# A chunked attention and feed-forward kernel: the first product of mm2 moved into mm1, mm2's other products in a new order

## Chip, cores, metric

One core of a Trainium2 chip runs the whole program. The metric is the device time of one execution in microseconds (us); lower is better. The kernel before took 271.1 us in the median of three runs (270.4 to 271.34).

## What is computed

Attention within chunks of 64 tokens, for 8 batches of 8 heads with 576 tokens of 64 features each, and behind it a feed-forward layer with an exact GELU over the 4608 tokens, 512 to 2048 to 512 features:

```python
q_c, k_c, v_c = (a.reshape(B, H, nc, chunk, D) for a in (q, k, v))
scores = scale * np.matmul(q_c, k_c.transpose(0, 1, 2, 4, 3))
attn = softmax(scores)
x = np.matmul(attn, v_c)            # brought to (B * S, H * D)
h = x @ w_in
g = 0.5 * h * (1.0 + erf(h / sqrt(2)))
out = g @ w_out
```

Inputs and output are float32; the matrix products take bf16 and add up in float32.

## The kernel before

**Tiles.** The tokens are cut into nine tiles of 512, t = 0 to 8. Tile t < 8 holds the first 512 tokens of batch t, tile 8 the last 64 of all eight batches. Each tile goes through attention (scores S, their exp, the product AV with the values, the division by the row sums, which gives x), then mm1 (x by w_in, and GELU, which gives h), then mm2 (h by w_out, which gives y). The program is written out in one order for each engine, and the engines meet through semaphores only. While tile t is in mm2, AV of tile t+1 and S of tile t+2 are run between its products.

**Seven products.** From tile 1 on in mm1 and from tile 3 on in mm2 the products are done by Strassen's scheme in Winograd's form: seven products of half blocks instead of eight, with sums of blocks before and after. In mm1 (`mm1_groups`) this is done for four groups a, b, c, d of features, so 28 products of 4 matmuls. Their order, with what ACT and DVE do between, is a string of words (`FOUR`, L638, for tiles 3 to 8): `3b` is the third product of group b; `c1b`, `c2b`, `c3b` copy a bank of group b; `a1b`, `a2b` add its bank Z onto such a copy; `g12b` is the GELU (on ACT) of one quarter of group b, where the digits are the half of the features and the half of the rows; `h1` to `h3` are parts of the sums s1 and s2 that mm2 takes (`h_sums`). a1d and a2d are the additions of group d. g21 and the GELUs of the same half give the blocks that mm2 calls h12.

**mm2** (`mm2_seven`) makes seven products of 16 matmuls into banks X, Y, Z and W of PSUM: X = h11 by w11; its copy to Y; Y += s2 by T2; X += h12 by w21; Y += s1 by T1; Z = h22 by T4; W = s3 by T3; Y += s4 by w22. T1 to T4 are sums of w_out's blocks. Between them ACT and DVE copy or add the banks into the output rows y and into the pieces s2 (tile `y_2`) and s5 (tile `y_5`), which are copies of Y at two moments. `also(i)` inserts the attention of other tiles: `also(1)` the AV of tile t+1 (`rows_av`) and its division (`rows_x`), `also(2)` the loads of later tiles and, between the two halves of a product (`(2, 0)`) or ahead of it (tile 3), S of tile t+2 (`quad_S`) with four exps on ACT.

**ACT's tables.** Exp and GELU are in different tables of ACT. `act_table` runs a tiny activation on a scratch tile, so that the load of the table stands at that place (`ACT_TABLE_LOAD`, then an activation of `act_scratch`): Exp ahead of AV, Gelu behind the exps.

**Banks.** PSUM's eight banks are three for products (`ps_mm`), two (`ps_tp`) and three (`ps_at`) for the rest. A bank is taken in rotation: X of mm2 gets the one that mm1's group b had for its Y, Z that of group d. AV needs six banks at once: two, three and, as the last, Z of the tile in mm2 (`rows_av(n, tiles[n - 1]["Z"])`). S then reuses four of the first five.

**Queues.** All loads and stores but a few at the end are issued by SP in program order; `rows_x` issues two DMA transposes there, which bring x into the layout for mm1.

Of the kernel before, what the change touches and what calls it, by code (L numbers as in the profile page):

```python
# [11 lines left out]
def kernel(  # L12
# [10 lines left out]
    P = 128  # L23
# [328 lines left out]
    def rows_x(t):  # L352

        st = tiles[t]
        rows = work.tile([P, 2, 2 * G, 2, D], bf16, tag="x_t", name="x_r", bufs=1)
        xT = by_halves(t).rearrange("p s g (n e) -> p s (g n) e", e=P)
        for bank in range(6):
            s, b0 = bank // 3, NX * (bank % 3)
            nb = min(NX, 2 * G - b0)
            av = st["av"][bank][:, :2 * nb]  # L360
            one = work.tile([P, 2 * NX], f32, tag="one", name="one", bufs=2)
            nc.vector.reciprocal(one[:, :2 * nb], av[:, :, D])
            nc.vector.tensor_tensor(rows[:, s, b0:b0 + nb].rearrange("p b r d -> p (b r) d"), av[:, :, :D],
                                    one[:, :2 * nb].to_broadcast([P, 2 * nb, D]), op=mybir.AluOpType.mult)
            if bank % 3 == 2:
                nc.sync.dma_start_transpose(xT[:, s], rows[:, s].rearrange("p b r d -> p (b r d)"))

    def duo_banks(g2, name):
# [203 lines left out]
    def h_sums(t, j0, j1):  # L572

        a11, a12, a21, a22 = h_blocks(t, j0, j1)
        s1, s2 = h_sum(t, 1, j0, j1), h_sum(t, 2, j0, j1)
        nc.vector.tensor_tensor(s1, a21, a22, op=mybir.AluOpType.add)
        nc.vector.tensor_tensor(s2, s1, a11, op=mybir.AluOpType.subtract)
# [37 lines left out]
    def x_sums(t, which=(1, 3, 2, 4)):  # L615
# [7 lines left out]
        for i in which:  # L623
# [16 lines left out]
               g12a c1d 2b a2a g22b 6d 5c g21a a2b 2d 7c h1 g11b c3c c2d 2c g11d 5d a1c 7d c3d 3c g21b 4c g11c 3b a1d  # L640
               g22c 4d g12c g12b 3d a2c a2d g21c g22d g12d g21d h2 h3"""

    FOURS = range(FIRST7, NT)
    PROGRAMS = {1: LATE, 2: THIRD, **{t: FOUR for t in FOURS}}

    def mm1_groups(t, extra, between={}):

        st = tiles[t]
        st["h"] = hpool.tile([P, FF, MT], bf16, tag="h", name="h")
        h = st["h"][:].rearrange("p f (m e) -> p f m e", m=2)  # L650
        b11, b12, b21, b22 = x_blocks(t)
        w = in_blocks()
        TT, add = nc.vector.tensor_tensor, mybir.AluOpType.add
        banks, sums = {}, {}
        four = t in FOURS
        tags = {"a": ("y_1", "y_2"), "b": ("y_5", "rc" if four else "y_2"), "d": ("y_1", "rc")}
        first = {"a": 0, "b": 4, "c": 2, "d": 6}
        plain = [] if four else [j + FH * r for j in (6, 7) for r in range(2)]
        hs = {"h1": (0, 2), "h2": (2, 6), "h3": (6, 8)}

        def prod(g, n):
            q, e = first[g] // 4, first[g] % 4
            if n in (1, 2):
                lhs, rhs, name = w[:, n - 1, :, 0, q, e:e + 2], b11 if n == 1 else b21, "X"
            elif n == 3:
                lhs, rhs, name = w_s[g, 4], b22, "Y"
            elif n == 4:
                lhs, rhs, name = w[:, 1, :, 1, q, e:e + 2], st["T"][4], "Z"
            else:
                lhs, rhs, name = w_s[g, n - 4], st["T"][n - 4], "Z" if n == 7 else "Y"  # L670
            fresh = n in (1, 7)
            if fresh:
                pool, tag = (ps_tp, "tp") if four and name == "Z" else (ps_at, "at")
                banks[g + name] = pool.tile([P, 2, TH], f32, tag=tag, name=f"h_{name}")
            for i in range(2):
                for kk in range(2):
                    nc.tensor.matmul(banks[g + name][:, i], lhs[:, kk, i], rhs[:, kk], start=fresh and i == kk == 0,  # L677
                                     stop=(kk == 1), skip_group_check=True)

        def gelu(g, r, m):  # L680
            j = first[g] + FH * r
            src = {(0, 0): lambda: banks[g + "X"], (0, 1): lambda: banks[g + "Y"],
                   (1, 0): lambda: sums[g, 0], (1, 1): lambda: sums[g, 1]}[r, m]()
            nc.scalar.activation(h[:, j:j + 2, m], src[:], Act.Gelu)  # L684

        for word in PROGRAMS.get(t, PROGRAM).split():
            for u in extra.pop(word, ()):
                u()
            if word == "start":
                begun = mm1_slot(t, [plain.pop(0) for _ in range(4)], between, 1)  # L690
            elif word == "sums":
                x_sums(t)
            elif word == "p" and t == 1:
                begun.pop()()
            elif word == "p":
                f = plain.pop(0)
                bank = ps_tp.tile([P, MT], f32, tag="tp", name="h_ps")
                for ks in range(KS):
                    nc.tensor.matmul(bank[:].rearrange("p (s e) -> p s e", s=2), w_in_sb[:, ks, f * P:(f + 1) * P],  # L699
                                     by_halves(t)[:, :, ks] if t >= FIRSTX else  # L700
                                     st["x"][:, ks, :].rearrange("p (s e) -> p s e", s=2),
                                     start=(ks == 0), stop=(ks == KS - 1))
                nc.scalar.activation(st["h"][:, f, :], bank[:], Act.Gelu)
            elif word in hs:
                if t >= FIRST7:
                    h_sums(t, *hs[word])
            elif word[0].isdigit():
                prod(word[1], int(word[0]))
            elif word[0] == "g":
                gelu(word[3], int(word[1]) - 1, int(word[2]) - 1)  # L710
            elif word[:2] == "c1":
                g = word[2]
                banks[g + "Y"] = ps_mm.tile([P, 2, TH], f32, tag="mm", name="h_Y")
                AC(banks[g + "Y"][:], banks[g + "X"][:])  # L714
            elif word[:2] in ("c2", "c3"):
                g, i = word[2], int(word[1]) - 2
                if g != "c":
                    tag = tags[g][i]
                    sums[g, i] = work.tile([P, 2, TH], f32, tag=tag, name=f"h_{g}", bufs=2 if tag == "rc" else 1)
                elif i == 0:  # L720
                    pool, tag = (hsum, "s3") if t < B else (ypool, "y")
                    pair = pool.tile([P, 4, TH], f32, tag=tag, name="h_sb")
                    sums[g, 0] = pair[:, 0:2]
                    sums[g, 1] = pair[:, 2:4]
                (AC if i == 0 else DV)(sums[g, i][:], banks[g + "Y"][:])  # L725
            elif word[0] == "a":
                g, i = word[2], 2 - int(word[1])
                TT(sums[g, i][:], banks[g + "Z"][:], sums[g, i][:], op=add)
# [29 lines left out]
    def halves(bank):  # L758
        return [bank[:, 0], bank[:, 1]]

    def mm2_seven(t, at={}):

        def also(i):
            for u in at.get(i, ()):
                u()
        st = tiles[t]
        h = st["h"][:].rearrange("p (k f) (m e) -> p k f m e", k=2, m=2)
        w = w_out_sb[:].rearrange("p (k f) (n e) -> p k f n e", k=2, n=2)
        T = [None] + [w_t[i] for i in range(1, 5)]
        def bank_mm():  # L770
            return ps_mm.tile([P, 2, NH], f32, tag="mm", name="y_ps")
        X, Y = bank_mm(), bank_mm()
        s2, s5 = (work.tile([P, 2, NH], f32, tag=nm, name=nm, bufs=1) for nm in ("y_2", "y_5"))
        y = [ypool.tile([P, 2, d_model], f32, tag="y", name="y_sb") for _ in range(2)]
        TT, add = nc.vector.tensor_tensor, mybir.AluOpType.add
        if t == B:
            s1 = work.tile([P, 2, NH], f32, tag="y_1", name="y_1", bufs=1)
            last_seven(t, h, w, T, (X, Y, bank_mm()), (s1, s2, s5), y)
            return
        also(0)  # L780
        product(halves(X), h[:, 0, :, 0], w[:, 0, :, 0], True)
        AC(Y[:], X[:])  # L782
        Z = bank_mm()
        st["Z"] = Z[:].rearrange("p m n -> p (m n)")
        also(1)
        h_third(t)
        product_by_f(halves(Y), h_sum(t, 2), T[2])
        AC(s2[:], Y[:])
        product(halves(X), h[:, 1, :, 0], w[:, 1, :, 0], False)
        AC(y[0][:, :, :NH], X[:])  # L790
        store(t, 0, 0, y)
        product(halves(Y), h_sum(t, 1), T[1], False)
        AC(s5[:], Y[:])
        h_fourth(t)
        also(2)
        product(halves(Z), h[:, 1, :, 1], T[4], True, lambda m: also((2, m)))
        TT(s2[:], Z[:], s2[:], op=add)
        also(3)
        W = bank_mm()
        product(halves(W), h_sum(t, 3), T[3], True)  # L800
# [164 lines left out]
    with tc.manual_schedule():  # L965
# [126 lines left out]
        for t in range(1, NT):  # L1092
# [30 lines left out]
            elif n < NT:  # L1123
# [58 lines left out]
                    e2[4] += [next_k]  # L1182
                if n + 1 < NT:
                    e2[1] = [lambda: act_table(Act.Exp)] + e2[1]
                    e2.setdefault(2 if t == FIRST7 else (2, 0), []).extend([lambda: quad_S(n + 1), lambda: act_table(Act.Gelu)])
            phase(t, e1, e2, between=last_rows if t == 1 else {})
# [1 line left out]
_INS = ['q', 'k', 'v', 'moe_w_in', 'moe_w_out']  # L1188
# [26 lines left out]
```

## Time and profile before

| | us |
|---|---|
| median of three runs | 271.1 |
| lowest, highest | 270.4, 271.34 |
| the profiled execution, device time | 270.41 |
| its span, first to last instruction | 268.6 |
| tile 4, from its first product of mm1 to that of tile 5 | 134.66 to 160.93 |
| mean clock granted to TensorE | 0.996 of full speed |

PE is TensorE's matmuls, PEld its loads of weights, DVE VectorE, ACT ScalarE, POOL GpSimd, SP the engine that issues DMAs. A row of a timeline has its start and its length in us, the engine, the line of the kernel, the operation, output<-inputs, shape and count; in brackets the time that the engine sat idle before, and who ended it. Rows of equal kind that follow each other are merged. In the chain of waits the program is followed back from its last instruction, each step to what released it.

### The profile page before, as it was taken

To read this page: it belongs to the slowest core of one execution; us is meant where nothing else is said; L and a number is where in the kernel's file an instruction comes from. 1 tells how busy PE (TensorE), PEld (TensorE's weight loads), DVE (VectorE), ACT (ScalarE), POOL (GpSimd) and SP (SyncE) were. 2 spreads that over 40 slices of the span, in tenths; PEclk is the share of its full clock that TensorE was granted. 3 is DMA by queue.
4 is the path that set the end of the run, shared out by engine and by line. 5 is a ranking of instruction groups with operands and counts; after the bars stand their busy time and mean duration, and the time that the engine had idled before them with its cause. 6 is when DMAs were issued, how large, how long until landed. Compare 5 with 4: busy or idle time off the path is not lost.

```text
span 268.6 us, 7554 instructions
## 1 busy us (share of the span) xinstructions
PE 259.6 (97%) x3077; PEld 195.6 (73%) x3092; DVE 202.1 (75%) x372; ACT 187.1 (70%) x364; POOL 77.0 (29%) x130
## 2 busy tenths in 40 slices
PE   7989999999999999999999999999999999999993
PEld 3554454476548654888888888888888888888882
DVE  2565775989997879589569956995699769958961
ACT  3466756797767967897689669957995799239700
POOL 3735667361440061441044103500362030000000
PEclk9999999999999999999999999999999999999998
DMA  7999999997979959999899989988886760430005
GB/s 230 285 377 402 395 388 243 237 286 194 336 205 261 244 123 231 279 237 191 232 232 231 177 216 242 264 152 206 237 193 146 166 192 0 89 138 12 2 2 156
DMA packets 127075, 56.59 MB, mean 211 GB/s; under 512 B 103488, under 2 KB 120896, under 8 KB 127040
## 3 DMA queue, kind: packets, MB, share of 16 engines
q1 hardware_dynamic: 126592, 55.59, 79.4%
q10 hardware_dynamic: 448, 0.52, 0.7%
q8 instruction: 24, 0.39, 0.6%
q14 instruction: 11, 0.09, 0.1%
HBM read 36.70 MB, written 9.44 MB: 172 GB/s over the span
## 4 chain that ended last, share of the span: by engine, by line
PE 92%; ACT 2%; DVE 1%; DMA 1%; issue 1%; POOL 0%; SPq 0%; ACTq 0%; DVEq 0%; POOLq 0%
PE y_ps L746 24%; PE h_Y L677 15%; PE y_ps L866 12%; PE h_Z L677 10%; PE h_X L677 10%; PE h_ps L538 6%; PE y_ps L891 4%; PE y_ps L755 4%; PE s_ps L247 2%; PE h_ps L699 1%; DMA arrival<-in_k_dram 1%; PE tp L170 1%; ACT y_ps L782 1%; PE warm L958 1%; PE rc_ps L484 1%
## 5 line engine op out<-in xcount | busy, mean ns | idle before, releaser
L677 PEld LDWEIGHTS <-w_in_s 128*128 128x128 bf16 x480 | 46.8, 98 | 6.1
L677 PEld LDWEIGHTS <-w_in_sb 128*128 128x128 bf16 x360 | 35.1, 98 | 6.5
L677 PE MATMUL h_X<-x,w_in_sb 128*128 128x256 bf16 x240 | 33.7, 272 | 0.0
L677 PE MATMUL h_Y<-x_t,w_in_s 128*128 128x256 bf16 x240 | 32.7, 272 | 0.0
L866 PE MATMUL y_ps<-w_out_sb,h 128*128 128x512 bf16 x137 | 31.7, 379 | 0.9 <-issue 0.8
L746 PEld LDWEIGHTS <-h_s 128*128 128x128 bf16 x304 | 29.7, 98 | 3.6 <-issue 0.2
L746 PEld LDWEIGHTS <-h 128*128 128x128 bf16 x288 | 27.8, 98 | 3.4
L218 POOL CAST v_nat<-arrival 128x1024 bf16<-128x1024 f32 x14 | 14.8, 1061 | 48.4 <-DMA arrival<-in_v_dram 48.3
L164 POOL CAST q_nat<-arrival 128x512 bf16<-128x512 f32 x33 | 19.4, 627 | 28.2 <-DMA arrival<-in_q_dram 19.1
L164 POOL CAST k_nat<-arrival 128x512 bf16<-128x512 f32 x34 | 21.9, 678 | 14.0 <-DMA arrival<-in_k_dram 10.1
L746 PE MATMUL y_ps<-w_t,h_s 128*128 128x256 bf16 x208 | 24.8, 273 | 0.0
L866 PEld LDWEIGHTS <-h 128*128 128x128 bf16 x144 | 13.3, 98 | 15.0 <-issue 0.2
L746 PE MATMUL y_ps<-w_out_sb,h 128*128 128x256 bf16 x192 | 22.9, 273 | 0.0
L963 ACT ACT_TABLE_LOAD x16 | 20.5, 1283 | 1.0 <-PEq L1199 0.7
L684 ACT ACTIVATE h<-h_Y 128x512 bf16<-128x512 f32 x30 | 17.7, 595 | 2.4 <-PE h_Y L677 1.9
L714 ACT COPY h_Y<-h_X 128x512 f32<-128x512 f32 x30 | 17.0, 582 | 2.8 <-PE h_X L677 2.6
L684 ACT ACTIVATE h<-h_X 128x512 bf16<-128x512 f32 x30 | 17.8, 597 | 1.4 <-PE h_X L677 0.6
L677 PE MATMUL h_Z<-x_t,w_in_s 128*128 128x256 bf16 x120 | 18.0, 273 | 0.0
L677 PE MATMUL h_Y<-x,w_in_s 128*128 128x256 bf16 x120 | 17.7, 273 | 0.0
L677 PE MATMUL h_Z<-x_t,w_in_sb 128*128 128x256 bf16 x120 | 17.4, 272 | 0.0
L725 DVE COPY h_a<-h_Y 128x512 f32<-128x512 f32 x8 | 5.5, 692 | 14.1 <-PE h_Y L677 14.1
L254 ACT ACTIVATE pT<-s_ps 128x512 bf16<-128x512 f32 x28 | 14.5, 601 | 2.3 <-PE s_ps L247 2.3
(148 smaller groups left out, 489.4 us busy)
## 6 DMA issues: line engine op xcount, KB each, us to landing
arrival<-in_q_dram SPq DMA_DIRECT2D x7, 1024.0 KB
arrival<-in_k_dram SPq DMA_DIRECT2D x24, 256.0 KB
out_dram<-y_sb SPq DMA_DIRECT2D x23, 256.0 KB
arrival<-in_v_dram SPq DMA_DIRECT2D x20, 256.0 KB
arrival<-in_moe_w_out_dram SPq DMA_DIRECT2D x4, 1024.0 KB
arrival<-in_v_dram SPq DMA_DIRECT2D x30, 128.0 KB
out_dram<-y_sb SPq DMA_DIRECT2D x5, 512.0 KB
arrival<-in_moe_w_in_dram SPq DMA_DIRECT2D x4, 512.0 KB
```

The costliest lines, as they stand in the source:

```text
L164: copy(st[nm][:, g].rearrange("p j r d -> p r j d"), st[nm + "f"][:, 2 * g:2 * g + 2])
L218: copy(st["v"][:, part[0], part[1], :D], st["vf"][:, part[0], part[1]])
L254: nc.scalar.activation(pT[:].rearrange("p u (c j) -> p u c j", j=J), s_ps[g2][c][:].rearrange("p u (j c) -> p u c j", j=J), Act.Exp, scale ...
L538: nc.tensor.matmul(h_ps[a][:], w_in_sb[:, ks, f * P:(f + 1) * P], st["x"][:, ks, :], start=(ks == 0), stop=(ks == KS - 1))
L677: nc.tensor.matmul(banks[g + name][:, i], lhs[:, kk, i], rhs[:, kk], start=fresh and i == kk == 0, stop=(kk == 1), skip_group_check=True)
L684: nc.scalar.activation(h[:, j:j + 2, m], src[:], Act.Gelu)
L714: AC(banks[g + "Y"][:], banks[g + "X"][:])
L746: nc.tensor.matmul(out[m], lhs[:, f, m * P:(m + 1) * P], rhs[:, f, :], start=fresh and f == 0 and (m == 0 or len(out) == 3), stop=(f == FH ...
L755: nc.tensor.matmul(out[m], lhs[:, f, m * P:(m + 1) * P], rhs[:, f, :], start=False, stop=(f == FH - 1), skip_group_check=True)
L866: nc.tensor.matmul(y_ps[:], st["h"][:, f, ms * P:(ms + 1) * P], w_out_sb[:, f, :], start=(f == 0), stop=(f == FF - 1))
L891: nc.tensor.matmul(tiles[t]["y_ps", ms][:], tiles[t]["h"][:, f, ms * P:(ms + 1) * P], w_out_sb[:, f, :], start=(f == 0), stop=False)
L963: nc.scalar.activation(act_scratch[:], rest[:, 0:1], func)
```

## The change

It touches tiles 3 to 7 (tile 8 keeps its order).

- **mm1's words.** A new string `AHEAD` stands for `FOUR`. It differs in its last third: 3b comes ahead of 3c, then 4c, and then `X`, the whole product h11 by w11 of mm2 (16 matmuls), ahead of 4d and 3d. `cX` copies X to Y on ACT, behind g21c. On DVE the sums of `h2` come ahead of a2d.
- **mm2's order.** PE's products were X, AV, Y += s2 T2, X += h12 w21, Y += s1 T1, Z (with S between its halves), W, Y += s4 w22. Now they are X += h12 w21, AV, Y += s2 T2, Z, Y += s1 T1 (with S between its halves, in tile 3 too), W, Y += s4 w22. The store of the first half of y now comes ahead of the transposes on SP.
- **rows_x** reads AV's banks in the order 5, 3, 4, 0, 1, 2 instead of 0 to 5, and so issues the transpose of the second half of the rows first.

```diff
-        for bank in range(6):
+        for at, bank in enumerate((5, 3, 4, 0, 1, 2)):
...
-            if bank % 3 == 2:
+            if at % 3 == 2:
                 nc.sync.dma_start_transpose(xT[:, s], rows[:, s].rearrange("p b r d -> p (b r d)"))
...
+    AHEAD = """begin 1a 1b c1a 1c 6a 7a c1b c2a 6b 5a 2a c1c 6c c2b 5b 7b c3a g11a a1a c3b c2c 3a a1b 1d 4a g22a 4b
+               g12a c1d 2b a2a g22b 6d 5c g21a a2b 2d 7c h1 g11b c3c c2d 2c g11d 5d a1c 7d c3d 3b g21b g11c 3c a1d
+               g22c 4c g12b X g12c a2c 4d g22d g21c cX h2 a2d 3d g12d g21d h3"""
...
-    PROGRAMS = {1: LATE, 2: THIRD, **{t: FOUR for t in FOURS}}
+    PROGRAMS = {1: LATE, 2: THIRD, **{t: AHEAD if t < B else FOUR for t in FOURS}}
...
+            elif word == "X":
+                mm2_first(t)
+            elif word == "cX":
+                st["Y"] = bank_mm()
+                AC(st["Y"][:], st["X"][:])
...
+    def mm2_first(t):
+        h, w = out_blocks(t)
+        tiles[t]["X"] = bank_mm()
+        product(halves(tiles[t]["X"]), h[:, 0, :, 0], w[:, 0, :, 0], True)
+
     def mm2_seven(t, at={}):
...
-        X, Y = bank_mm(), bank_mm()
+        X, Y = (st["X"], st["Y"]) if t < B else (bank_mm(), bank_mm())
...
-        also(0)
-        product(halves(X), h[:, 0, :, 0], w[:, 0, :, 0], True)
-        AC(Y[:], X[:])
         Z = bank_mm()
         st["Z"] = Z[:].rearrange("p m n -> p (m n)")
+        product_by_f(halves(X), h[:, 1, :, 0], w[:, 1, :, 0])
+        AC(y[0][:, :, :NH], X[:])
+        store(t, 0, 0, y)
         also(1)
-        h_third(t)
         product_by_f(halves(Y), h_sum(t, 2), T[2])
         AC(s2[:], Y[:])
-        product(halves(X), h[:, 1, :, 0], w[:, 1, :, 0], False)
-        AC(y[0][:, :, :NH], X[:])
-        store(t, 0, 0, y)
-        product(halves(Y), h_sum(t, 1), T[1], False)
-        AC(s5[:], Y[:])
+        product(halves(Z), h[:, 1, :, 1], T[4], True)
+        h_third(t)
+        TT(s2[:], Z[:], s2[:], op=add)
         h_fourth(t)
         also(2)
-        product(halves(Z), h[:, 1, :, 1], T[4], True, lambda m: also((2, m)))
-        TT(s2[:], Z[:], s2[:], op=add)
+        product(halves(Y), h_sum(t, 1), T[1], False, lambda m: also((2, m)))
+        AC(s5[:], Y[:])
         also(3)
...
-                    e2.setdefault(2 if t == FIRST7 else (2, 0), []).extend([lambda: quad_S(n + 1), lambda: act_table(Act.Gelu)])
+                    e2.setdefault((2, 0), []).extend([lambda: quad_S(n + 1), lambda: act_table(Act.Gelu)])
```

ACT in mm2 of tile 4, before (y_2 is s2, y_5 is s5, pT are the exps of S, y_sb the output rows; y_ps are banks X and Y):

```order
L782 COPY y_ps_2706<-y_ps_2705 128x512
L963 ACT_TABLE_LOAD
L963 ACTIVATE act_scratch_113<-rest_58 128x1
L788 COPY y_2_2707<-y_ps_2706 128x512
L790 COPY y_sb_2709<-y_ps_2705 128x2x256
L793 COPY y_5_2708<-y_ps_2706 128x512
L254 ACTIVATE pT_2968<-s_ps_2900 128x512
L254 ACTIVATE pT_2970<-s_ps_2901 128x512
L254 ACTIVATE pT_2972<-s_ps_2902 128x512
L254 ACTIVATE pT_2974<-s_ps_2903 128x512
L963 ACT_TABLE_LOAD
L963 ACTIVATE act_scratch_113<-rest_58 128x1
```

The same place with the change (line numbers are the changed file's):

```order
L801 COPY y_sb_2726<-y_ps_2686 128x2x256
L978 ACT_TABLE_LOAD
L978 ACTIVATE act_scratch_113<-rest_58 128x1
L805 COPY y_2_2724<-y_ps_2711 128x512
L254 ACTIVATE pT_2968<-s_ps_2900 128x512
L254 ACTIVATE pT_2970<-s_ps_2901 128x512
L254 ACTIVATE pT_2972<-s_ps_2902 128x512
L254 ACTIVATE pT_2974<-s_ps_2903 128x512
L978 ACT_TABLE_LOAD
L978 ACTIVATE act_scratch_113<-rest_58 128x1
L812 COPY y_5_2725<-y_ps_2711 128x512
L821 COPY y_sb_2726<-y_ps_2711 128x2x256
```

The copy of X to Y has left (it stands between two GELUs of mm1 now), and the copy into y_5 has gone from ahead of the exps to behind the table load and its scratch activation.

DVE at the end of mm1 of tile 4, before (h_d is group d's piece, h_sb group c's; h_s1 and h_s2 are the sums s1 and s2):

```order
L728 TENSOR_TENSOR h_sb_2590<-h_Z_2634,h_sb_2590 128x512
L728 TENSOR_TENSOR h_d_2650<-h_Z_2662,h_d_2650 128x512
L576 TENSOR_TENSOR h_s1_2639<-h_2513 128x1024
L577 TENSOR_TENSOR h_s2_2640<-h_s1_2639,h_2513 128x1024
L576 TENSOR_TENSOR h_s1_2639<-h_2513 128x512
L577 TENSOR_TENSOR h_s2_2640<-h_s1_2639,h_2513 128x512
L362 RECIPROCAL one_2800<-av_ps_2730 128x6
```

And with the change:

```order
L737 TENSOR_TENSOR h_sb_2590<-h_Z_2634,h_sb_2590 128x512
L576 TENSOR_TENSOR h_s1_2639<-h_2513 128x1024
L577 TENSOR_TENSOR h_s2_2640<-h_s1_2639,h_2513 128x1024
L737 TENSOR_TENSOR h_d_2650<-h_Z_2662,h_d_2650 128x512
L576 TENSOR_TENSOR h_s1_2639<-h_2513 128x512
L577 TENSOR_TENSOR h_s2_2640<-h_s1_2639,h_2513 128x512
L362 RECIPROCAL one_2818<-y_ps_2728 128x4
```

a2d (h_d_2650) has gone behind the two sums of `h2`, and the first bank that the division reads is now Z (y_ps_2728).

More of the change, by code (lines that the diff above doesn't have):

```diff
@@ L759, in halves, with bank_mm, out_blocks @@
         return [bank[:, 0], bank[:, 1]]
+    def bank_mm():
+        return ps_mm.tile([P, 2, NH], f32, tag="mm", name="y_ps")
+    def out_blocks(t):
+        return (tiles[t]["h"][:].rearrange("p (k f) (m e) -> p k f m e", k=2, m=2),
+                w_out_sb[:].rearrange("p (k f) (n e) -> p k f n e", k=2, n=2))
+    def mm2_first(t):
+        h, w = out_blocks(t)
+        tiles[t]["X"] = bank_mm()
+        product(halves(tiles[t]["X"]), h[:, 0, :, 0], w[:, 0, :, 0], True)
     def mm2_seven(t, at={}):
@@ L766, in mm2_seven @@
         st = tiles[t]
-        h = st["h"][:].rearrange("p (k f) (m e) -> p k f m e", k=2, m=2)
-        w = w_out_sb[:].rearrange("p (k f) (n e) -> p k f n e", k=2, n=2)
+        h, w = out_blocks(t)
         T = [None] + [w_t[i] for i in range(1, 5)]
-        def bank_mm():
-            return ps_mm.tile([P, 2, NH], f32, tag="mm", name="y_ps")
-        X, Y = bank_mm(), bank_mm()
+        X, Y = (st["X"], st["Y"]) if t < B else (bank_mm(), bank_mm())
         s2, s5 = (work.tile([P, 2, NH], f32, tag=nm, name=nm, bufs=1) for nm in ("y_2", "y_5"))
```

## The prediction

> **What bounds the kernel now.** I read the page's busy times and its chain that ended last, then the table of stretches (one per tile), then the timelines of PE, ACT and DVE for tile t = 4, the second of the five that change.
>
> ```profile
> PE 259.6 (97%) x3077; PEld 195.6 (73%) x3092; DVE 202.1 (75%) x372; ACT 187.1 (70%) x364; POOL 77.0 (29%) x130
> PE 92%; ACT 2%; DVE 1%; DMA 1%; issue 1%; POOL 0%; SPq 0%; ACTq 0%; DVEq 0%; POOLq 0%
> 134.70:161.00 26.30, 26.25 (x355) 23.09 (x353) 20.22 (x41) 20.68 (x37) 7.05 (x12) 1.00 1.02 212
> 213.60:239.10 25.50, 25.45 (x290) 22.53 (x289) 20.13 (x41) 15.64 (x29) 2.10 (x2) 1.00 0.37 93
> ```
>
> The first two rows say that PE is the bound: 92% of the chain is PE. The other two are stretches (start:end, length, then busy time of PE, PEld, DVE, ACT, POOL, then granted clock, DMA share, GB/s): PE is busy 26.25 of 26.30 us at clock 1.00. So nothing is to be won by filling large holes; a change gains tenths by closing small gaps, and it loses whatever new wait it puts in front of PE. ACT is busy for only 20.68 us, so what matters on ACT is the order, not the sum.
>
> The PE timeline of t = 4 (start, length, line, operation):
>
> ```profile
> 144.81 0.60 PE L677 MATMUL h_Y<-x,w_in_s 128*128 128x256 bf16 x4
> 145.24 0.60 PE L677 MATMUL h_Z<-x_t,w_in_sb 128*128 128x256 bf16 x4
> 145.68 0.60 PE L677 MATMUL h_Y<-x,w_in_s 128*128 128x256 bf16 x4
> 146.18 0.60 PE L677 MATMUL h_Z<-x_t,w_in_sb 128*128 128x256 bf16 x4
> 146.61 0.60 PE L677 MATMUL h_Y<-x,w_in_s 128*128 128x256 bf16 x4
> 147.05 1.91 PE L746 MATMUL y_ps<-w_out_sb,h 128*128 128x256 bf16 x16
> 148.89 0.60 PE L347 MATMUL av_ps<-v_nat,pT 64*64 64x65 bf16 x50
> ...
> 149.67 1.91 PE L755 MATMUL y_ps<-w_t,h_s 128*128 128x256 bf16 x16
> 154.91 1.04 PE L746 MATMUL y_ps<-w_t,h 128*128 128x256 bf16 x8
> 155.88 0.74 PE L247 MATMUL s_ps<-q_t,k_t 64*64 64x64 bf16 x64
> 156.55 1.05 PE L746 MATMUL y_ps<-w_t,h 128*128 128x256 bf16 x8
> 157.43 1.91 PE L746 MATMUL y_ps<-w_t,h_s 128*128 128x256 bf16 x16
> 159.18 1.91 PE L746 MATMUL y_ps<-w_out_sb,h_s 128*128 128x256 bf16 x16
> ```
>
> Starts give the pace: a product of mm1 (4 matmuls) takes 0.435, one of mm2 (16) takes 1.75 (157.43 to 159.18), so a matmul 0.109. A length is longer than the pace because matmuls overlap. Gaps: 3b to 4d is 0.50 in place of 0.44; the scores S cost 0.76 (from 154.91 + 0.875 = 155.79 to 156.55); AV costs 0.87 (147.05 + 1.75 = 148.80 to 149.67).
>
> **The change part by part.** I work in the frame of this tile: nothing of mm1 moves before 144.81.
>
> *What it may gain.* Before, AC(Y<-X) stands between X and the product on Y:
>
> ```profile
> 145.44 0.60 ACT L684 ACTIVATE h<-h_Y 128x512 bf16<-128x512 f32 x1
> 146.32 0.60 ACT L684 ACTIVATE h<-h_Y 128x512 bf16<-128x512 f32 x1 [0.28 <-PE h_Y L677]
> 147.85 0.59 ACT L684 ACTIVATE h<-h_Y 128x512 bf16<-128x512 f32 x1
> 148.33 0.63 ACT L684 ACTIVATE h<-h_d 128x512 bf16<-128x512 f32 x1
> 149.05 0.57 ACT L782 COPY y_ps<-y_ps 128x512 f32<-128x512 f32 x1
> ```
>
> The copy ends at 149.62 and the product on Y starts at 149.67: PE had finished AV and waited. With X and its copy in mm1 that wait goes. AV should then cost what S costs, whose 64 matmuls are as many: 0.76, so 0.11 a tile (bounds 0 and 0.15). The 0.06 ahead of 4d goes too: 4d overwrites the bank that a1d reads until 146.12 (DVE rows below), and X now stands between them.
>
> *X inside mm1.* The order is 3b 3c 4c X 4d 3d, so 3b starts at 144.81, 3c at 145.24, 4c at 145.68, X at 146.12. X's bank was group b's, which g12b reads: 3b ends at 144.81 + 0.60 = 145.41, g12b starts 0.03 later as the second ACT row does after its product (145.68 + 0.60 = 146.28), and ends at 146.04. X is not held (0.03 to spare once 0.05 for the signal is counted, 149.62 to 149.67). X runs to 147.87, 4d to 148.31, 3d to 148.75.
>
> *The product onto X, now first in mm2* (h12 by w21, at 148.75). It needs two things early. First the copy of X: X's last matmul ends at 146.12 + 1.91 = 148.03, the copy started 0.09 after that end before (147.05 + 1.91 = 148.96, 149.05), so it runs 148.12 to 148.69 and releases PE at 148.74, just in time. Second, from its 13th matmul on (148.75 + 12 x 0.109 = 150.06), g21d, which waits for a2d on DVE, which now stands behind the sums of h2:
>
> ```profile
> 145.43 0.69 DVE L728 TENSOR_TENSOR h_d<-h_Z,h_d 128x512 f32<-128x512 f32 x1
> 146.04 0.68 DVE L728 TENSOR_TENSOR h_sb<-h_Z,h_sb 128x512 f32<-128x512 f32 x1
> 147.42 0.68 DVE L576 TENSOR_TENSOR h_s<-h 128x1024 bf16<-128x1024 bf16 x1
> 148.14 0.69 DVE L577 TENSOR_TENSOR h_s<-h_s,h 128x1024 bf16<-128x1024 bf16 x1
> 149.54 0.19 DVE L362 RECIPROCAL one<-av_ps 128x6 f32<-128x6 f32 x1
> 153.07 0.42 DVE L363 TENSOR_TENSOR x_r<-y_ps,one 128x256 bf16<-128x256 f32 x1
> 153.41 1.21 DVE L581 TENSOR_TENSOR h_s<-h 128x2048 bf16<-128x2048 bf16 x1
> 159.44 0.69 DVE L801 TENSOR_TENSOR y_sb<-y_ps,y 128x512 f32<-128x512 f32 x1 [1.04 <-PE y_ps L746]
> 160.64 0.75 DVE L625 TENSOR_TENSOR x_t<-x 128x512 bf16<-128x512 bf16 x2
> ```
>
> a2c waits for 4c (ends 146.28) and runs to 147.01; h2 takes the next 1.33 (147.42 to 148.75 in these rows), to 148.26; a2d needs 4d's end, 147.87 + 0.60 = 148.47, and runs to 149.20. On ACT, g12d waits for 3d (ends 148.91), starts at 148.94, and g21d follows at the usual step of 0.48 (147.85 to 148.33), 149.42 to 150.05. With 0.05 for the signal and 0.11 for the weights, the 13th matmul starts at 150.21 and not 150.06: **0.15 lost**. Bounds: 0 (ACT a little ahead) and 0.7 (a2d late by one more DVE operation).
>
> So AV starts 0.15 later, ends 0.11 faster, and 0.06 is already won: S stands where it stood, 155.88, and the five tiles win or lose nothing here: -0.02 each.
>
> *Reading the banks.* The twelve operations of rows_x keep their 3.87 (149.54 to 153.41) but start after AV's end, about 151.4, and end at 155.3. Bank 5 is free at 152.0, the product on Z comes at 153.16. S reuses banks that are read by 154.6, before 155.88. The third sum then ends at 156.5 (wanted 157.43), the fourth, behind one addition more, at 158.3 (wanted 159.18). All covered; by 0.9 at the least.
>
> *s5: the copy that changes its place.* Before, AC(s5<-Y) ran ahead of the exps. Now Y's product with s1 is the one around S, so in ACT's order its copy stands behind the four exps, the load of the Gelu table and the scratch activation:
>
> ```profile
> 155.11 0.59 ACT L793 COPY y<-y_ps 128x512 f32<-128x512 f32 x1 [1.16 <-PE y_ps L746]
> 156.38 2.06 ACT L254 ACTIVATE pT<-s_ps 128x512 bf16<-128x512 f32 x4 [0.68 <-PE s_ps L247]
> 158.46 1.28 ACT L963 ACT_TABLE_LOAD   x1
> 159.76 0.20 ACT L963 ACTIVATE act_scratch<-rest 128x1 f32<-128x1 bf16 x1
> 77.00 0.20 ACT L963 ACTIVATE act_scratch<-rest 128x1 f32<-128x1 bf16 x1
> 77.11 1.05 ACT L877 COPY y_sb<-y_ps 128x512 f32<-128x512 f32 x2
> ```
>
> S starts at 155.88 as before, so exps, load and scratch keep these times. The last two rows, from an earlier tile, show that a copy starts 0.11 after the scratch's start: s5 runs 159.87 to 160.46. The last product of the tile adds onto Y, so it may not start before Y is read: 160.51 and not 159.18. **PE waits 1.33**, in the tiles that have an S here (t = 3 to 6; t = 7 has no tile left to score and no table to load). Behind it on ACT stand the last copy and next tile's copies of X, which wait for PE anyway; on DVE the two additions to y and x_sums start at 160.5, not 159.44, and give T2 some 2.3 later (1.20 from the first addition to x_sums in the rows above, then three sums), at 162.8; PE wants it after the last product and three of mm1, 160.51 + 1.75 + 1.31 = 163.6. Nothing is added to the wait, and nothing gives it back: mm1 that follows is PE-bound (25.45 of 25.50 in the tile without S). Bounds: 1.22 (first exp 0.1 sooner) and 1.45.
>
> The Trainium skill, "ScalarE: Activation LUTs", section "What ACT_TABLE_LOAD costs", puts a switch of sets at about 1283 ns of load and 1380 ns of drain. By it the wait would be 1.33 + 1.38 = 2.71 and the sum four times 1.38, 5.5, larger. The load agrees with the row 158.46; of the drain the rows 159.76 and 77.11, which follow at once, show nothing.
>
> *Sum:* 4 x 1.33 - 5 x 0.02 = +5.2. Profiled execution: 270.4 (span 268.6, 1.8 around it) to 275.6. The median before, 271.1, lies 0.7 above that execution; **I predict 276.3**.
>
> **Rivals.**
> *The wait does not decide (other side).* The place is Y's last product in t = 3 to 6. Its copy must end 3.25 after S's start and ends 4.58 after it; the difference is the table load, 1.28, almost exactly. If the load ran beside the exps, or the copy came ahead of it, the wait would be 0.05. With g21d in time too, the tiles would win 0.17 each: 271.1 + 0.2 - 0.9 = 270.4. For it speaks only that ACT has idle time; against it that load and exps stand one behind another in the rows, as everything on ACT does.
> *g21d later than worked out.* From about 0.15, each tenth is paid five times. At the bound of 0.7, 276.3 + 5 x 0.55 = 279.0. The chain has four handovers between ACT and DVE, which speaks for something; but it starts from 4c, early.
> *The transposes of x become late.* They wait for rows_x, so come 1.9 later:
>
> ```profile
> 147.89 1.20 SPq L144 DMA_DIRECT2D arrival<-in_v_dram  x2
> 151.63 3.50 SPq L366 DMA_TRANSPOSE x<-x_r  x2
> ```
>
> Issued by 155.13, they had landed at 160.64, when x_sums started unheld: within 5.5. Now they are out by 157.0 and wanted at 161.7 (160.64 plus the 1.0 that DVE starts later): 4.7. If the whole 5.5 is needed, 0.8 in four tiles and up to 1.9 in the fifth: 276.3 + 5.1 = 281.4 at most, 278.5 at half. SP idles ahead of them (149.09 to 151.63), which speaks against a queue. The loads behind them come 1.9 later too, a tile or more before use.
> *The table load stalls ACT after it as well.* If it took as long again as its row, 1.28, the wait would be 2.61 four times: 281.4. The rows 77.00 and 77.11 speak against it. This is where the page of the skill points.
>
> **How the numbers follow.** Forecast 0.82; g21d clearly later 0.07; transposes 0.04; long load 0.02; no wait at Y 0.05. The forecast's own range is 4 x (1.22 to 1.45) with the tile's small terms from -0.17 to +0.25 five times, +4.0 to +7.0: 275.1 to 278.1. With the medians' own scatter (270.4 to 271.34) and part of the second rival, 274.7 to 278.3 holds 8 in 10. What a measurement here can tell from no change is about 0.3%, 0.8 us. Faster 0.03 and same 0.03, nearly all from the rival on the other side; slower 0.94.
>
> **What would show it.** Right: in t = 3 to 6 a PE gap of about 1.3 ahead of the last product on Y, released by the ACT copy into y_5, which starts right after the scratch activation; none in t = 7; the copy of X off the chain of waits; a gap of 0.1 to 0.2 within the first product of mm2. Wrong: that copy ahead of the exps, a gap after the load, x_sums waiting for DMA, or tiles no longer than 26.3.

## The result, and the profile after

| | before | after |
|---|---|---|
| median of six runs, us | 271.35 | 275.44 |
| lowest, highest, us | 270.4, 272.55 | 274.41, 277.25 |
| ratio of the times, 95% interval | 1 | 1.0156 [1.0116, 1.0197] |
| profiled execution, us | 270.41 | 275.05 |
| its span, us | 268.6 | 273.3 |

By the medians the kernel became slower by 4.1 us; the interval of the ratio makes it 3.1 to 5.3 us. Against the prediction (276.3, range 274.7 to 278.3) the time came out 0.9 lower and inside the range.

The page after, its busy times and the shares of its chain that ended last:

```profile
PE 260.1 (95%) x3077; PEld 194.6 (71%) x3092; DVE 202.6 (74%) x372; ACT 187.2 (69%) x364; POOL 77.5 (28%) x130
PE 77%; SPq 9%; DMA 5%; ACT 4%; issue 2%; POOL 2%; DVE 0%; POOLq 0%
```

PE's busy time grew by 0.5 us only (259.6 before), while the span grew by 4.7: the time went into PE standing still, not into more work. That the chain gives 9% to SP's queue looks like a new bound, but most of it is one place: followed back from the end, the chain leaves PE in tile 6 through a k_t that came late (below), and from there runs over POOL's casts of k and along the issue of loads in SP's queue from 199.83 back to 184.99. The table by tile says more. Its columns are start:end, length, busy time of PE, PEld, DVE, ACT and POOL, the granted clock, DMA share and GB/s; the tiles are cut at their first product of mm1. After the change:

```profile
107.82:135.31 27.49, 26.35 (x353) 22.92 (x352) 20.00 (x38) 20.35 (x37) 6.79 (x11) 1.00 0.97 227
135.31:162.82 27.51, 26.37 (x355) 22.93 (x353) 20.27 (x40) 20.67 (x37) 7.07 (x12) 1.00 0.91 209
...
190.33:218.19 27.86, 26.43 (x355) 22.90 (x353) 20.76 (x40) 20.66 (x37) 8.15 (x14) 1.00 0.91 184
218.19:243.68 25.49, 25.49 (x290) 22.20 (x288) 19.98 (x39) 15.74 (x29) 2.10 (x2) 1.00 0.33 85
sum 135.86, PE 131.01 PEld 113.88 DVE 101.25 ACT 98.09 POOL 30.01; mean PE 26.20 PEld 22.78 DVE 20.25 ACT 19.62 POOL 6.00
```

The same cut before the change:

```profile
108.40:134.66 26.26, 26.21 (x354) 23.05 (x352) 19.54 (x37) 20.26 (x37) 6.86 (x11) 1.00 0.99 236
...
187.19:213.53 26.34, 26.29 (x354) 22.96 (x352) 21.43 (x40) 20.68 (x37) 8.34 (x14) 1.00 0.75 183
sum 130.62, PE 130.39 PEld 114.65 DVE 101.34 ACT 97.94 POOL 30.11; mean PE 26.08 PEld 22.93 DVE 20.27 ACT 19.59 POOL 6.02
```

Tiles 3, 4 and 5 (27.49, 27.51, 27.51) are 1.23 to 1.25 longer, tile 6 is 1.52 longer, and tile 7, the one without scores to compute, has its old 25.49. The sum is +5.24. The two profiled executions differ by less, 4.64, because in the one of after the tiles begin 0.58 earlier (107.82 for 108.40). The program is unchanged up to there, so that part is scatter between executions.

Where it goes within a tile is in PE's timeline of t = 4 after the change:

```profile
146.33 0.60 PE L681 MATMUL h_Z<-x_t,w_in_sb 128*128 128x256 bf16 x4
146.77 1.91 PE L755 MATMUL y_ps<-w_out_sb,h 128*128 128x256 bf16 x16
...
149.39 1.98 PE L764 MATMUL y_ps<-w_out_sb,h 128*128 128x256 bf16 x16
151.30 0.60 PE L347 MATMUL av_ps<-v_nat,pT 64*64 64x65 bf16 x50
...
152.00 1.92 PE L764 MATMUL y_ps<-w_t,h_s 128*128 128x256 bf16 x16
...
156.47 0.74 PE L247 MATMUL s_ps<-q_t,k_t 64*64 64x64 bf16 x64
157.14 2.79 PE L755 MATMUL y_ps<-w_t,h_s 128*128 128x256 bf16 x24
161.07 1.91 PE L755 MATMUL y_ps<-w_out_sb,h_s 128*128 128x256 bf16 x16 [1.14 <-ACT y L812]
```

The row of 24 matmuls is the second half of Y's product and all of W's. At the prediction's pace, 1.75 for 16 matmuls, it is done at 157.14 + 24 x 0.1094 = 159.77, and the last product onto Y starts at 161.07: PE waits 1.30 (the bracket's 1.14 counts only from the end of the last matmul). The same bracket stands in t = 3, 4, 5 and 6, and nowhere else. ACT in the same stretch, and then the chain of waits there:

```profile
156.97 2.06 ACT L254 ACTIVATE pT<-s_ps 128x512 bf16<-128x512 f32 x4 [2.38 <-PE s_ps L247]
159.05 1.28 ACT L978 ACT_TABLE_LOAD   x1
160.35 0.20 ACT L978 ACTIVATE act_scratch<-rest 128x1 f32<-128x1 bf16 x1
160.46 0.57 ACT L812 COPY y<-y_ps 128x512 f32<-128x512 f32 x1
```

```profile
156.54 0.45 PE s_ps L247 x30
156.98 2.05 ACT pT L254 x4
...
160.55 0.48 ACT y L812
161.07 1.91 PE y_ps L755 x16
```

Y's product was complete by about 158.2 (157.14 and its eight matmuls, 0.875, with the overlap), yet the copy that frees Y has four exps and a table load ahead of it in ACT's order. It does not need either of them; it merely stands behind them. PE leaves its own work at the scores, goes through ACT and comes back 1.30 late.

### The profile page after: what moved, and what is told of

It reads as the page before. It is cut to its first block, busy times and chain, and to the rows that moved or that the text cites. A ratio compares the mean times of both kernels' runs of the same rounds, so it can differ in the third digit from the quotient of the medians.

```text
span 273.3 us, 7553 instructions
## 1 busy us (share of the span) xinstructions
PE 260.1 (95%) x3077; PEld 194.6 (71%) x3092; DVE 202.6 (74%) x372; ACT 187.2 (69%) x364; POOL 77.5 (28%) x130
## 4 chain that ended last, share of the span: by engine, by line
PE 77%; SPq 9%; DMA 5%; ACT 4%; issue 2%; POOL 2%; DVE 0%; POOLq 0%
PE y_ps L755 15%; PE h_Y L681 13%; PE y_ps L881 11%; PE h_Z L681 9%; PE h_X L681 8%; PE h_ps L538 5%; PE y_ps L764 5%; PE y_ps L906 4%; DMA arrival<-in_moe_w_in_dram 3%; SPq L106 2%; ACT pT L254 2%; DMA k_t<-k_nat 2%; SPq L149 2%; SPq L111 2%; PE s_ps L247 2%
## 5 line engine op out<-in xcount | busy, mean ns | idle before, releaser
L881 PEld LDWEIGHTS <-h 128*128 128x128 bf16 x144 | 13.4, 98 | 15.0 <-issue 0.2
L755 PEld LDWEIGHTS <-h 128*128 128x128 bf16 x208 | 20.4, 98 | 2.3
L978 ACT ACT_TABLE_LOAD x16 | 20.5, 1283 | 1.0 <-PEq L1214 0.7
L681 PE MATMUL h_Y<-x,w_in_s 128*128 128x256 bf16 x120 | 16.9, 272 | 0.0
L755 PE MATMUL y_ps<-w_out_sb,h_s 128*128 128x256 bf16 x96 | 11.4, 272 | 4.6 <-ACT y L812 4.6
```

The source lines that it names most:

```text
L755: nc.tensor.matmul(out[m], lhs[:, f, m * P:(m + 1) * P], rhs[:, f, :], start=fresh and f == 0 and (m == 0 or len(out) == 3), stop=(f == FH ...
L881: nc.tensor.matmul(y_ps[:], st["h"][:, f, ms * P:(ms + 1) * P], w_out_sb[:, f, :], start=(f == 0), stop=(f == FF - 1))
L978: nc.scalar.activation(act_scratch[:], rest[:, 0:1], func)
```

## The experiments

Each kernel was timed beside the kernel before on the same chip, whose median over those runs was 270.72 (17 runs, first four experiments) and 270.52 (23 runs, last four). Diffs are against the changed kernel where nothing else is said.

**1. The table load behind the copy.** If the 1.28 of the load are the whole loss, putting the load behind the copy of s5 must give everything back.

```diff
-                    e2.setdefault((2, 0), []).extend([lambda: quad_S(n + 1), lambda: act_table(Act.Gelu)])
+                    e2.setdefault((2, 0), []).append(lambda: quad_S(n + 1))
+                    e2[3].append(lambda: act_table(Act.Gelu))
```

> The changed kernel with the Gelu table's load (and its scratch activation) moved behind the copy of s5; the copy still stands behind the four exps. Theory (the load ahead of the copy is what holds Y's last product): copy ends about 3.7 after S starts less the 0.6 that exps leave, that is at 159.6 in the changed kernel's tile 4, before PE comes at 159.77; the four waits of 1.30 go, tiles 3 to 5 take 26.2 each, 275.4 - 5.2 = 270.3. In tile 6 S also waits for k_t (0.36 in the changed kernel); that chain runs over SP and POOL and does not shorten, so there up to 1.3 of the gain may come back: up to 271.6. Rival (the exps, or the fourth sum on DVE, hold it): 274 or more, and a gap before Y's last product stays.

Measured: 270.47 us (12 runs), ratio to before 0.9998 [0.9968, 1.0028]. ACT and PE of t = 4 in this kernel:

```profile
156.04 2.06 ACT L254 ACTIVATE pT<-s_ps 128x512 bf16<-128x512 f32 x4 [2.38 <-PE s_ps L247]
157.97 0.62 ACT L812 COPY y<-y_ps 128x512 f32<-128x512 f32 x1
158.60 1.28 ACT L978 ACT_TABLE_LOAD   x1
```

```profile
156.21 2.79 PE L755 MATMUL y_ps<-w_t,h_s 128*128 128x256 bf16 x24
158.84 1.91 PE L755 MATMUL y_ps<-w_out_sb,h_s 128*128 128x256 bf16 x16
```

The copy ends at 158.59, the product onto Y follows its predecessor without a bracket (156.21 + 2.63 = 158.84), and tiles 3 to 7 add up to 130.61 us, where before had 130.62. So the order of the load and the copy is all of the loss, and the rest of the change together is worth nothing that can be measured (the interval is -0.9 to +0.8 us).

**2. Two more switches in the same place.** This stretches the disputed cost, and asks whether a load holds ACT longer than its row says.

```diff
-                    e2.setdefault((2, 0), []).extend([lambda: quad_S(n + 1), lambda: act_table(Act.Gelu)])
+                    e2.setdefault((2, 0), []).extend([lambda: quad_S(n + 1), lambda: act_table(Act.Gelu),
+                                                      lambda: act_table(Act.Exp), lambda: act_table(Act.Gelu)])
```

> The changed kernel with one more switch to Exp and one more to Gelu (two loads and two scratch activations) between the exps and the copy of s5, in tiles 3 to 6. Theory: each adds its own rows, 1.28 + 0.20 + 0.03 = 1.5, so the wait grows from 1.30 to 4.3 and the time by 4 x 3.0 = 12.0, to 287.4. Rival of a load that also stalls ACT after it (1.38 more each by the Trainium skill's figure, ScalarE: Activation LUTs, What ACT_TABLE_LOAD costs): 4 x 5.8 = 23, to 298.5. If the copy did not decide: 275.4.

Measured: 294.9 us (2 runs), ratio 1.0887 [1.0826, 1.0947], 7.5 more than forecast. ACT of t = 3 with the extra switches:

```profile
131.72 1.28 ACT L978 ACT_TABLE_LOAD   x1
133.01 0.20 ACT L978 ACTIVATE act_scratch<-rest 128x1 f32<-128x1 bf16 x1
133.23 1.28 ACT L978 ACT_TABLE_LOAD   x1
...
134.75 1.28 ACT L978 ACT_TABLE_LOAD   x1
136.04 0.20 ACT L978 ACTIVATE act_scratch<-rest 128x1 f32<-128x1 bf16 x1
136.15 0.57 ACT L812 COPY y<-y_ps 128x512 f32<-128x512 f32 x1
```

Each switch, load and scratch, takes 1.51 (131.72, 133.23, 134.75), with nothing behind the load that holds ACT. PE's row, and the windows of its wait and of the product behind:

```profile
136.77 3.49 PE L755 MATMUL y_ps<-w_out_sb,h_s 128*128 128x256 bf16 x16 [4.17 <-ACT y L812]
```

```profile
132.50:136.70 4.20, 0.10 (x1) 0.00 (x0) 0.00 (x0) 4.13 (x7) 0.00 (x0) 1.00 1.05 313
136.70:140.10 3.40, 3.33 (x17) 2.32 (x17) 3.32 (x6) 0.02 (x1) 2.56 (x4) 0.53 0.69 157
```

The row of 24 matmuls ahead starts at 129.80, so the wait is 136.77 - 132.43 = 4.34, which is 1.30 + 2 x 1.52. That part is as expected. What the expectation left out is the granted clock, the third number from the right: 1.00 during the wait, 0.53 in the stretch after it. The last product then takes 3.28 (136.77 to 140.05) in place of 1.75. With 1.61, 1.45 and 1.61 in the other three tiles that is 6.2. In t = 4 and 6 the slow stretch reaches into mm1 as well, as its first row behind t = 4 shows (1.47 at full clock):

```profile
172.32 2.51 PE L681 MATMUL h_X<-x,w_in_sb 128*128 128x256 bf16 x12
```

By their starts, these 12 matmuls take 1.04 longer behind t = 4, 0.79 behind t = 6 and 0.13 behind t = 3, 2.0 together. Tiles 3 to 7 add up to 155.97, 20.1 more than after the change: 12.0 for the switches, 6.2 and 2.0 for the clock.

**3. The banks read in their old order.** This undoes `rows_x` alone, to see what the reversal is for.

```diff
-        for at, bank in enumerate((5, 3, 4, 0, 1, 2)):
+        for at, bank in enumerate(range(6)):
```

> The changed kernel with rows_x reading AV's banks in the order 0 to 5 again. Theory: the product on Z, due 1.75 after AV, now waits for the last of twelve DVE operations (3.9 from AV's end) and not for the first two (0.6): about 2.0 in each of five tiles, 285.4, with the wait for s5 unchanged at 1.3. Rival (DVE gets there in any case, since it can start on bank 0 before AV is over): 276 to 278.

Measured: 286.18 us (2 runs), ratio 1.0565 [1.0506, 1.0623]; the forecast is 0.8 off. In t = 4 the product on Z waits for the last read of AV's last bank:

```profile
158.85 1.91 PE L755 MATMUL y_ps<-w_t,h 128*128 128x256 bf16 x16 [1.85 <-DVE x_r L363]
```

The product ahead starts at 155.07, so it was due at 156.82: 2.03 lost. Without that bank read first, Z in the middle of mm2 costs 2 us a tile. The edit costs all five tiles, t = 7 as well, as this wait does not hang on the scores.

**4. The kernel before with its copy of s5 late.** The mechanism alone, without anything else of the change: one line of the kernel before moves behind the product on Z, which puts it behind the scores' exps.

```diff
         product(halves(Y), h_sum(t, 1), T[1], False)
-        AC(s5[:], Y[:])
...
         product(halves(Z), h[:, 1, :, 1], T[4], True, lambda m: also((2, m)))
+        AC(s5[:], Y[:])
```

> The kernel before with one line moved: the copy of s5 goes behind the product on Z, so that on ACT it stands behind the exps, the Gelu load and the scratch activation, as the change has it. Everything else as before. Theory: this alone makes nearly all of the loss. In tiles 4 to 6 S stands as far ahead of Y's last product as in the change: 1.30 each; in tile 3 S comes one half product earlier, so 1.30 - 0.87 = 0.43; sum 4.3, to 275.6. Rival (the loss comes from the order of PE or from late transposes): 271.3.

Measured: 274.34 us (5 runs), 3.6 over before, ratio 1.0136 [1.0097, 1.0175]. PE and then ACT of t = 4:

```profile
156.58 1.91 PE L746 MATMUL y_ps<-w_t,h_s 128*128 128x256 bf16 x16
159.62 1.91 PE L746 MATMUL y_ps<-w_out_sb,h_s 128*128 128x256 bf16 x16 [1.13 <-ACT y L796]
```

```profile
159.00 0.57 ACT L796 COPY y<-y_ps 128x512 f32<-128x512 f32 x1
```

The product was due at 156.58 + 1.75 = 158.33 and starts 1.29 later. Tiles 3 to 6 grow by 0.41, 1.28, 1.30 and 1.21; in t = 3 the scores still stand ahead of the product on Z, so the copy has more time. With experiment 1 this closes the case from both sides: the copy behind exps and load makes the loss without the change, and the change with the load moved behind the copy makes none.

**5. The load behind the copy, and g21d ahead of g12d.** The first experiment with the one other small loss removed, as a candidate that could beat both. The edit of experiment 1 is in it too; shown is what it adds.

```diff
-               g22c 4c g12b X g12c a2c 4d g22d g21c cX h2 a2d 3d g12d g21d h3"""
+               g22c 4c g12b X g12c a2c 4d g22d g21c cX h2 a2d 3d g21d g12d h3"""
```

> The changed kernel with the Gelu load behind the copy of s5, and on ACT g21d ahead of g12d. Theory: g21d is then issued at a2d's end (149.87 in the changed kernel's tile 4) and not behind g12d (150.08), and ends 0.2 earlier, so the 0.07 that PE loses at the 13th matmul of the first product of mm2 goes in each of five tiles: 0.3 less than with the load moved alone, about 270.1 against 270.5; tiles 26.13. Too little for the times to settle; the tiles' lengths in the trace should show it. Rival: g12d, now later, holds the sums of h3 or AV's last bank, and the gap comes back there: tiles 26.2 or longer.

Measured: 270.53 us (12 runs), ratio 1.0003 [0.9977, 1.0029]. The table by tile of this kernel, its sum:

```profile
sum 130.17, PE 130.10 PEld 114.29 DVE 101.78 ACT 98.01 POOL 29.39; mean PE 26.02 PEld 22.86 DVE 20.36 ACT 19.60 POOL 5.88
```

The five tiles take 0.45 less than before (t = 3, 5 and 6 take 26.12 to 26.14; t = 4 takes 26.35, as X starts 0.2 late there). mm2's first product isn't held any more (149.20 to 151.04 in t = 4, its pace and the 0.09 in front of AV), but the gain is within the scatter of the times (269.95 to 272.05). No version tried here is faster than before.

**6. One more switch.** Between the wait of 1.3 that leaves the clock alone and the one of 4.3 that does not.

```diff
-                    e2.setdefault((2, 0), []).extend([lambda: quad_S(n + 1), lambda: act_table(Act.Gelu)])
+                    e2.setdefault((2, 0), []).extend([lambda: quad_S(n + 1), lambda: act_table(Act.Sqrt),
+                                                      lambda: act_table(Act.Gelu)])
```

> The changed kernel with one more table load (a square root on the scratch tile) between the exps and the Gelu load, in tiles 3 to 6. PE's wait becomes 1.30 + 1.5 = 2.8 (4.3 with two more loads, after which the granted clock fell to 0.53 for some 3 us). Theory: the wait alone is paid, 275.4 + 4 x 1.5 = 281.4, if the clock stays at 1.00 after 2.8; if the clock already falls after 2.8, some 1.7 more in the tiles where it does, up to 288.

Measured: 288.32 us (2 runs), ratio 1.066 [1.0588, 1.0732]. The wait is 2.8 (a bracket of 2.66, where 1.14 stands for 1.30). PE's rows of t = 3 and 4:

```profile
138.07 1.91 PE L755 MATMUL y_ps<-w_out_sb,h_s 128*128 128x256 bf16 x16 [2.66 <-ACT y L812]
167.19 3.37 PE L755 MATMUL y_ps<-w_out_sb,h_s 128*128 128x256 bf16 x16 [2.66 <-ACT y L812]
```

The windows of the second of these products and of what comes behind it:

```profile
167.20:170.40 3.20, 3.20 (x16) 2.26 (x16) 3.20 (x5) 0.00 (x0) 2.67 (x4) 0.53 1.20 270
170.40:173.00 2.60, 2.60 (x26) 2.31 (x24) 0.65 (x2) 2.14 (x5) 0.00 (x0) 1.00 0.76 173
```

After the first wait of 2.8 the product has its usual length, 1.91, and so the full clock; after the second it has 0.53, and 1.00 again 3.2 us later. In t = 5 and 6 it is as in t = 4 (lengths of 3.49 and 3.44). The tiles are 10.8 longer than after the change, and 4 x 1.5 for the loads with 1.46, 1.57 and 1.53 for the three slow products make 10.6. The profiled execution has 2.8 more ahead of tile 3, where the program is unchanged; what it is was not settled. Why the first of the four waits left the clock alone is taken up at the end.

**7. Only X moved into mm1.** mm2's remaining products go back to before's order, with s5 copied ahead of the scores.

```diff
-        product_by_f(halves(X), h[:, 1, :, 0], w[:, 1, :, 0])
-        AC(y[0][:, :, :NH], X[:])
-        store(t, 0, 0, y)
         also(1)
+        h_third(t)
         product_by_f(halves(Y), h_sum(t, 2), T[2])
...
-        product(halves(Z), h[:, 1, :, 1], T[4], True)
-        h_third(t)
-        TT(s2[:], Z[:], s2[:], op=add)
+        product(halves(X), h[:, 1, :, 0], w[:, 1, :, 0], False)
+        AC(y[0][:, :, :NH], X[:])
+        store(t, 0, 0, y)
+        product(halves(Y), h_sum(t, 1), T[1], False)
+        AC(s5[:], Y[:])
         also(2)
-        product(halves(Y), h_sum(t, 1), T[1], False, lambda m: also((2, m)))
-        AC(s5[:], Y[:])
+        product(halves(Z), h[:, 1, :, 1], T[4], True, lambda m: also((2, m)))
+        TT(s2[:], Z[:], s2[:], op=add)
```

> Only X and its copy stand in mm1 (with the new order of words and of banks); behind it mm2's products in the order of before: AV first, then s2, X by h12, s1 with its copy ahead of S, Z around S. Theory: no wait for s5, so the loss goes: the gain of the copy hidden in mm1 (0.08) and of the gap ahead of 4d (0.06) stands against AV, which now comes straight behind 3d and waits some 0.2 for a2d and g12d on two of its banks: 271.3, within 0.8. Rival (moving X in itself costs the time): 274 to 276.

Measured: 271.74 us (10 runs), ratio 1.0053 [1.0018, 1.0087]: a small loss. Tiles 3 to 6 take 105.93 us, 0.8 more than before (130.62 - 25.49 = 105.13). AV, now straight behind mm1, takes 1.00 in t = 4:

```profile
150.01 0.82 PE L347 MATMUL av_ps<-v_nat,pT 64*64 64x65 bf16 x50
...
151.01 1.92 PE L764 MATMUL y_ps<-w_t,h_s 128*128 128x256 bf16 x16
```

Before it was 0.78 (148.89 to 149.67). The row of 50 matmuls takes 0.82 where it took 0.60. The chain of waits shows where it stops:

```profile
150.08 0.31 PE av_ps L347 x24
150.39 0.03 issue
150.42 0.41 PE av_ps L347 x25
```

By the loops of `rows_av`, the 25th matmul is the first that writes the second of AV's banks, which group d's Z had and a2d reads until 150.37. In all five tiles the 25th starts 0.05 after a2d's end, 0.22 to 0.26 behind the 24th. The 51st, the first into the bank that g12d reads (until 150.72), starts at 150.76. These two holds, about 0.3 in all, are the wait that was expected (at some 0.2). So X in mm1 gains nothing by itself; the product h12 by w21 between mm1 and AV makes the move neutral, as it gives a2d and g12d the time.

**8. The scores between the halves of Z again.** The rest of the change stays, but the scores, and with them the exps and the load, stand one product earlier, so that s5's copy has 1.75 more.

```diff
-        product(halves(Z), h[:, 1, :, 1], T[4], True)
+        also(2)
+        product(halves(Z), h[:, 1, :, 1], T[4], True, lambda m: also((2, m)))
...
-        also(2)
-        product(halves(Y), h_sum(t, 1), T[1], False, lambda m: also((2, m)))
+        product(halves(Y), h_sum(t, 1), T[1], False)
```

> The changed kernel with S between the halves of the product on Z, where it stood before, and so 1.75 ahead of where the change has it; the copy of s5 still stands behind exps, load and scratch. Theory: Y's last product is now due 5.05 after S's start, later than the copy's end at 4.6, so the 1.30 goes; but S comes when DVE has read only some of AV's banks and its second half waits about 0.6: 275.4 - 4 x 0.7 = 272.8. Rival (the wait follows the copy wherever S stands): 275.

Measured: 276.04 us (4 runs), ratio 1.0218 [1.0157, 1.028]. This forecast, 272.8, missed. The last product onto Y isn't held any more, and tiles 4 and 5 take 26.87 and 26.86, as worked out. But in t = 3 and t = 6 the scores now come before their k_t has landed:

```profile
129.33 0.78 PE L247 MATMUL s_ps<-q_t,k_t 64*64 64x64 bf16 x64 [1.23 <-DMA k_t<-k_nat]
211.08 0.74 PE L247 MATMUL s_ps<-q_t,k_t 64*64 64x64 bf16 x64 [1.70 <-DMA k_t<-k_nat]
```

These tiles take 27.54 and 27.97, and t = 7 takes 25.89, 0.40 more than after the change, because mm1 behind t = 6 waits for a sum of x (x_t) on DVE. The five tiles together, 135.13, are 0.73 shorter than after the change. In the profiled execution they begin 0.81 later (108.63 for 107.82), where the program is the same, so that its span is 0.1 longer. That the median of the four runs (274.97 to 277.21) is 0.6 higher was not settled.

## Why the prediction was right

Point by point, by its own steps.

**s5, the copy that changes its place (1.33, four times): right.** Measured 1.30, in t = 3 to 6 and not in t = 7, released by the copy into y_5 that starts 0.11 after the scratch activation (160.35, 160.46), as the rows of the earlier tile had it. Experiments 1 and 4 show that it is the cause, experiment 2 that it grows by just the length of what is put in front.

**The small terms (-0.02 a tile): small, as said, but each a little off.** AV costs 0.70 (151.30 to 152.00) for 0.78, a gain of 0.08 where 0.11 was worked out. mm2's first product is held 0.07 by g21d (151.30 against 149.39 + 1.75 + 0.09), where 0.15 was: g21d ends at 150.70 and the 13th matmul starts at 150.76, so the 0.05 for the signal is there, but not the 0.11 for the weights. The 0.06 ahead of 4d went. That makes -0.07, and 1.30 - 0.07 = 1.23 is the growth of tile 3.

**X in mm1, the reads of the banks, the later sums: covered, as said, in the tiles with scores.** X starts at 146.77, one pace of 0.44 behind 4c and so unheld; the scores start 21.16 into the tile (156.47 - 135.31) where before had 21.22 (155.88 - 134.66). In t = 7 the third sum is not covered. No scores stand ahead of the product on W there, so it is due at 238.35 + 1.75 = 240.10; the sum ends at 240.13 and W starts at 240.18, 0.08 late. The margin had been worked out for a tile with scores.

**Nothing gives it back: right.** Tiles 4 and 5 lose their 1.24 again, and tile 7, which has no wait for s5, is as long as before (25.49): its small gain goes into the 0.08 ahead of W.

**The rivals.** "The wait does not decide" fell: load and exps stand one behind another. "g21d later" fell at 0.07. "The transposes of x become late" fell: x_sums starts at 162.26, straight behind the additions, with no wait for DMA. "The table load stalls ACT after it as well" fell in the trace after and once more in experiment 2. The Trainium skill, "ScalarE: Activation LUTs", section "What ACT_TABLE_LOAD costs", gives about 1283 ns of load, which every row here has, and 1380 ns of drain, which none of them shows: the next load follows a scratch activation 0.02 after its end.

**One sentence does not hold everywhere:** that the loads behind the transposes of x come "a tile or more before use". Those of k for tile 8 are issued from 193.24 on, behind the transposes of t = 5, and the scores in t = 6 want their k_t at 211.48, two thirds of a tile later. PE in t = 6 after the change, and the chain of waits there:

```profile
210.51 1.04 PE L755 MATMUL y_ps<-w_t,h_s 128*128 128x256 bf16 x8
211.84 0.74 PE L247 MATMUL s_ps<-q_t,k_t 64*64 64x64 bf16 x64 [0.28 <-DMA k_t<-k_nat]
```

```profile
206.16 5.63 DMA k_t<-k_nat
```

The scores were due at 211.48 (210.51 for the product ahead, 0.875 for its half, 0.09) and start 0.36 late, which is what tile 6 has over tiles 4 and 5. That the loads came later is not shown to be the cause. The transpose's issue isn't late: 15.83 into the tile (206.16 - 190.33), before 16.08 (203.27 - 187.19). It is the landing, 5.63, that is long; before it was within 5.21 (208.48 - 203.27), in experiment 1 within 3.71 (204.32 to 208.03). From issue to landing the DMA engines were busy for 0.94 of the time here, for 0.70 before (203.2 to 208.5) and for 0.81 in experiment 1 (204.3 to 208.1); why the landing varies was not tried. The prediction has no term for k_t, whose margin was thin, and experiment 8, which asked for k_t one product earlier still, failed on it.

**The total.** +5.24 in the tiles against +5.2; that it comes this close is partly luck. The waits for s5 make 5.20 (5.32 was worked out) and the small terms -0.28 (-0.10), 4.92 in all; the rest is, in the main, the late k_t of tile 6, which the prediction does not have. The timed difference of 4.1 is smaller. The runs of one kernel lie 2 to 3 us apart, whether each of them has the 0.36 of tile 6 is not shown, and the interval of 3.1 to 5.3 takes the +5.2 in only near its upper end.

## What to carry to other kernels

On an engine that works in order, moving a block of work past a copy moves the copy behind everything that this block issues there. Before such a move, list what then stands ahead of each instruction that frees a buffer, and set its sum against the time until the buffer is wanted: here 4.6 us of exps, load and copy stood against 3.3. Here the table load was the cheapest thing to put elsewhere: behind the copy it cost nothing that could be measured, ahead of it the whole 1.6%.

## What was not expected of the hardware

**The granted clock falls after shorter waits than assumed.** A wait of PE of 4.3 us brought the granted clock down to one half, and the product behind it took 3.28 in place of 1.75; this came in all four tiles of experiment 2 (lengths of 3.37 to 3.57 for 1.91), for 3.4 us in t = 3 and 5 and for 6.8 us in t = 4 and 6. After 2.8 it came in three of four (experiment 6), for 3.4 us. After 1.3 (after the change, experiment 4) and 2.03 (experiment 3) it never came. So a wait of 2.8 may cost 4.3 (with the 1.46 that the product from 167.19 to 170.40 took longer), which makes the loss of a long wait steeper than its length.

Finer windows of the same traces show which waits do it. The granted clock changes at 136.88, 140.30, 167.60, 174.43, 201.74, 205.15, 232.46 and 239.28 in experiment 2, and at 166.82, 170.23, 197.54, 200.95, 228.26 and 231.67 in experiment 6. Within a run these moments are whole multiples of 3.41 us apart. Cut into stretches of 3.41 at these moments, the seven stretches that end with a fall have PE idle for 2.29 us or more. The first wait of experiment 6 lies across such a border (136.10), 0.69 ahead of it and 1.97 behind it, and the clock stays. In t = 4 and 6 of experiment 2 the rest of the wait, 1.36 and 1.87, lies behind the border, and the clock comes back one stretch later. So in these two runs not the length of the wait counts, but how much of it falls into one stretch; the limit lies between 1.97 and 2.29 and was not tried more closely.

The Trainium skill, "TensorE: Matmul & The Clock Gate", "Part 1: The HAM clock gate", has the clock halved after at least one idle window of about 3.4 us, by a window that runs freely. The half rate and the stretches of 3.41 agree. If that means a window idle throughout, it does not agree: 2.29 us of idling in it were enough, and here the measurement decides.
